# The last two token groups of the second FFN run alternately, chunk by chunk, and three instead of four steps at the border between the FFNs are in reversed order

## The chip, the core and the metric

The kernel runs on one core of a Trainium2 chip. The core has TensorE (PE in the profile; its weight loads are PEld), VectorE (DVE), ScalarE (ACT), GpSimd (POOL) and SyncE (SP), which issues the transfers here. Each engine takes its instructions in the order in which they are written; semaphores tie the engines together. Matrix products land in PSUM (8 banks), everything else lies in SBUF. The metric is the device time of one execution in microseconds, as the median of several runs.

## The reference, cut to what matters

```python
def reference(...):
    attn_out = _attn_ref(q_l, k_l, v_l, q_g, k_g, v_g)      # windowed attention with global tokens
    x = attn_out.transpose(0, 2, 1, 3).reshape(B * S, H * D)   # 2176 x 512
    x = _moe_ref(x, w_in, w_out)
    return _moe2_ref(x, w_in, w_out, a, b)

def _moe_ref(x, w_in, w_out):            # first FFN, 512 -> 2048 -> 512
    h = x @ w_in
    r = np.maximum(h, 0.0)
    return ((r * r) @ w_out).astype(np.float32)

def _moe2_ref(x, w_in, w_out, a, b):     # second FFN, the same shapes
    h = x @ w_in
    P = a[0] + a[1] * h + a[2] * h**2 + a[3] * h**3
    Q = 1.0 + np.abs(b[0]) * np.abs(h) + np.abs(b[1]) * h**2
    return ((P / (Q + 1e-06)) @ w_out).astype(np.float32)
```

## The kernel before

Attention comes first, with part of the first FFN filled in beside it; then the rest of the first FFN and the whole second one run as a list of jobs. A job is one chunk `f` of 128 of the 2048 hidden features for one group of tokens. Every matrix operand is split into a rounded part, hi, and what is left, lo, and a product is three matmuls (hi by hi, hi by lo, lo by hi).

The second FFN (`ph` 1) has six groups: five of 384 tokens and a last one of 256, `GRP[1]`, with 16 chunks each. `jobs` lists them group by group. N1 is the number of the first job of the second FFN, and all its weights are in SBUF when it is under way.

`step(k)` writes what belongs to step k, and there is no other scheduler: each engine's queue is the order of the code.

- `do_h(k)`, L314: 12 matmuls, hidden chunk k in one of two PSUM banks named S. The weights are stationary and the tokens move, so their width is 384 or 256. It is called h below.
- `x_split`, L296 and L297: one of the four 128-feature slices of a group's input is split into hi (ScalarE) and lo (VectorE). It needs a free slot out of `x_free`. There are five slots in the buffer `big`; two more (`x_more`, tiles `xm`) lie in the four word buffers `T` through which weights were converted before, each of 128 x 512 words, two to a slot. `step` looks ahead by 10, 7, 4 and 1 jobs to the first job of a group and splits one slice, at a distance of 1 all that are missing. `do_h` gives the slots back at a group's last chunk.
- `do_y(j)` for the job three steps back, L394: for each block of 128 tokens three matmuls 512 wide into a y bank; hi and lo of the chunk's result are stationary. First come all that need hi, two for each block, then one for each block that needs lo: 9 matmuls for 384 tokens, 6 for 256. It is called y. Six banks serve y, three or two for a group, in turn.
- `rat_a(k)`: three ScalarE functions (L350 to L352) and three VectorE operations (L353 to L355) for the chunk just computed. `rat_b(k - 1)`: Ln and Exp on ScalarE (L362, L363), then three VectorE operations (L364 to L366). `rat_c(k - 2)`: the copy to hi on ScalarE (L372), then lo on VectorE (L373).
- After a group's last y its banks are copied out, three or two ScalarE copies (L415), and each copy is sent to DRAM by SP (L416).

Within a step the order is h, x_split, y, then the three `rat` calls, then the output copies. The `rat` calls stand in the order a, b, c, except in the first four steps of the second FFN, where c comes first:

```python
        rat = [lambda op=op, d=d: op(k - d) for d, op in enumerate((rat_a, rat_b, rat_c)) if N1 <= k - d < NJ]
        for op in rat[::-1] if k < N1 + 4 else rat:
            op()
```

Of the kernel before, what the change touches and what calls it, by code (L numbers as in the profile page):

```python
# [10 lines left out]
F32R = mybir.dt.float32r  # L11
# [12 lines left out]
def kernel(  # L24
# [24 lines left out]
    NK = DM // 128  # L49
# [9 lines left out]
    NMAX = 384  # L59
# [6 lines left out]
    def bank(tag):  # L66
        i = turns[tag].pop(0)
        turns[tag].append(i)
        return ps.tile([128, 512], F32, tag=f"b{i}", name=tag)
# [162 lines left out]
    def cv_tick(left):  # L232

        cv["z"] += 1
        for it in line:
            it["age"] += 1
        if cv["z"] >= cv["per"] and len(todo) > left:
            cv["z"] = 0
            it = todo.pop()
            if it["mode"] == "both":  # L240
                w_back(it)
            else:
                it["age"], it["at"] = 0, cv["at"] if it["mode"] == "wide" else OS
                w_load(it)
                line.append(it)
        for nm in ORD:
            for it in line:
                if it["at"].get(nm) == it["age"]:
                    OPS[nm.replace("el", "l")](it)
        line[:] = [it for it in line if it["age"] < it["at"]["lo"]]  # L250

    def cv_idle():
        return not (todo or line)
# [5 lines left out]
    def row(i, r, n):  # L259
        return rows[i][:, NMAX * r:NMAX * r + n]  # L260

    x_free = [0, 1, 2, 3, 4]
    x_more = {}

    def x_slot(n):
        i = x_free.pop(0)
        pair = x_more[i] if i in x_more else [row(0, 2 * i + z, NMAX) for z in range(2)]
        return i, [x[:, 0:n].bitcast(F32R) for x in pair]

    def h_slot(n):  # L270
# [4 lines left out]
    groups_of = [[], []]  # L275
    t0 = NPART
# [5 lines left out]
    t0 = 0  # L282
# [2 lines left out]
        t0 += n  # L285
    jobs = []
    for ph in range(2):
        for gi, (t0, n, fs, add) in enumerate(groups_of[ph]):
            for f in fs:
                jobs.append((ph, gi, t0, n, f, f == fs[0], f == fs[-1], add))  # L290
    xs = {}

    def x_split(ph, gi, t0, n, k):
        i, (hi, lo) = x_slot(n)
        src = xT[:, k, t0:t0 + n]
        sc.copy(hi, src)  # L296
        ve.tensor_tensor(out=lo, in0=src, in1=hi.bitcast(F32), op=ALU.subtract)  # L297
        xs[ph, gi, k] = hi, lo, i
        if k == NK - 1 and groups_of[ph][gi][3]:
            sy.dma_start(xT[:, :, t0:t0 + n], park[:, :, t0:t0 + n])  # L300
# [3 lines left out]
    def do_h(j):  # L304
        ph, gi, t0, n, f, _, last, _ = jobs[j]
        w = wt[ph, f]
        h = bank("S")[:, 0:n]
        wk = [[w[:, s, 0, 128 * k:128 * k + 128] for s in range(2)] for k in range(NK)]
        x = [xs[ph, gi, k] for k in range(NK)]
        mm = [(k, s, 0) for k in range(NK) for s in range(2)] + [(k, 0, 1) for k in range(NK)]  # L310
        if last:
            mm = [(k, s, t) for k in range(NK) for s, t in ((0, 0), (1, 0), (0, 1))]
        for m, (k, s, t) in enumerate(mm):
            pe.matmul(h, wk[k][s], x[k][t], start=m == 0, stop=m == 3 * NK - 1)  # L314
        if last:
            x_free.extend(xs.pop((ph, gi, k))[2] for k in range(NK))
        hps[j] = h

    gs, mid = {}, {}
# [5 lines left out]
    def relu2(j, spare_ve):  # L325
        n = jobs[j][3]
        h = hps.pop(j)
        (hi, lo), g = h_slot(n)
        sc.activation(g, h, AF.Relu)  # L329
        gs[j] = hi, lo  # L330

        def square():
            sc.activation(hi, g, AF.Square)  # L333
            if spare_ve:
                sc.activation(g, g, AF.Square)
            else:
                ve.tensor_tensor(out=g, in0=g, in1=g, op=ALU.mult)  # L337

        def rest():
            ve.tensor_tensor(out=lo, in0=g, in1=hi.bitcast(F32), op=ALU.subtract)  # L340

        return square, rest
# [35 lines left out]
    def do_y(j):  # L378
        ph, gi, t0, n, f, st, sp, add = jobs[j]
        hi, lo = gs.pop(j)  # L380
        w = wt[ph, f]
        if st:
            yb[ph, gi] = [bank("y") for _ in range(NK if ph == 0 else n // 128)]
        y = yb[ph, gi]

        ms = range(len(y))
        for m, z in [(m, z) for m in ms for z in range(2)] + [(m, 2) for m in ms]:
            c = slice(128 * m, 128 * m + 128)
            if ph == 0:
                a, x = w[:, z % 2, 1, c], (hi, hi, lo)[z]  # L390
                pe.matmul(y[m][:, 0:n], a, x, start=st and z == 0, stop=sp and z == 2)  # L391
            else:
                a, x = (hi, hi, lo)[z][:, c], w[:, z % 2, 1]
                pe.matmul(y[m], a, x, start=st and z == 0, stop=sp and z == 2)  # L394

        def evac1(m):
            o = xT[:, m, t0:t0 + n]
            if add:
                ve.tensor_tensor(out=o, in0=y[m][:, 0:n], in1=o, op=ALU.add)
            else:  # L400
                (sc.copy if m % 2 else ve.tensor_copy)(o, y[m][:, 0:n])  # L401

        def evac():
            if ph == 0:
                for m in range(NK):
                    if j == N1 - 1 and m:
                        held.append(lambda m=m: evac1(m))
                    else:
                        evac1(m)
            else:  # L410
                for m in range(n // 128):

                    ks, c = ((slice(0, 2), 0), (slice(2, 4), 0), (slice(0, 4), 256))[m]
                    o = xT[:, ks, t0 + c:t0 + c + (128 if c else 256)]
                    sc.copy(o, y[m].rearrange("p (k t) -> p k t", t=o.shape[2]))  # L415
                    sy.dma_start(out[t0 + 128 * m:t0 + 128 * m + 128, :].rearrange("p (k t) -> p k t", t=o.shape[2]), o)  # L416

        if sp:
            outs.append(evac)

    NJ = len(jobs)
    N1 = sum(j[0] == 0 for j in jobs)
# [3 lines left out]
    def step(k):  # L426
        last, late = False, []

        if k < NR + 3:
            ticks, stage = (6 - (k > 5) if len(todo) > LEFT[2] else 2), (2 if k < NF else 3)  # L430
        elif k < N1 - (NF - NPRE) + 3:
            ticks, stage = 2, 4
        else:
            ticks, stage = (0 if cv_idle() else 6), 5
        left = LEFT[stage]
        if k < NJ:
            ph, gi, t0, n, f, _, last, _ = jobs[k]
            while (ph, f, 1) not in done:
                cv_tick(left)
            do_h(k)  # L440
        if k == N1:
            wide_s.close()
            pools["t"] = ctx.enter_context(tc.tile_pool(name="tmp", bufs=2, side="right"))
        if k >= N1 and not x_more and cv_idle():
            for i in (5, 6):
                x_more[i] = [cv3.tile([128, 512], U32, tag="T", name="xm").bitcast(F32) for _ in range(2)]
                x_free.append(i)
        for d in (1, 4, 7, 10):
            if k + d < NJ and jobs[k + d][5]:
                for z in range(NK):  # L450
                    if jobs[k + d][:2] + (z,) not in xs and x_free:
                        x_split(*jobs[k + d][:4], z)
                        if d > 1:
                            break


        lag = [2 if y < N1 else 3 for y in ys[:2]]
        if ys and ys[0] <= k - lag[0]:
            do_y(ys.pop(0))
            lag.pop(0)  # L460
        while ys and (ys[0] <= k - lag[0] or (last and lag[0] == 2 and ys[0] < k)):
            do_y(ys.pop(0))
            lag.pop(0)
            lag.append(2 if ys and ys[0] < N1 else 3)
        if k < NJ:
            if ph == 0:
                late = list(relu2(k, k < NF))
                ys.append(k)
        rat = [lambda op=op, d=d: op(k - d) for d, op in enumerate((rat_a, rat_b, rat_c)) if N1 <= k - d < NJ]
        for op in rat[::-1] if k < N1 + 4 else rat:  # L470
            op()
        if N1 <= k - 2 < NJ:
            ys.append(k - 2)
        while outs:
            outs.pop(0)()
        if held and k >= N1 + 6:
            held.pop(0)()

        for t in range(ticks):
            if late and t == 1:  # L480
                late.pop(0)()
            cv_tick(left)
        for f in late:
            f()


    fs = ctx.enter_context(ExitStack())
# [60 lines left out]
    with ExitStack() as at:  # L548
# [329 lines left out]
        for i in range(NS + 1):  # L878
# [13 lines left out]
            late = i + 2 < NS and groups[i + 2][1] == 4  # L892
# [30 lines left out]
            elif 0 <= fq < len(fjobs) - NPRE:  # L923
                a, f = fjobs[fq]
# [59 lines left out]
```

## Time and profile before

| | us |
|---|---|
| median of 3 runs (941.53 to 942.43) | 942.24 |
| profiled execution, its own time | 942.59 |
| its span, first to last instruction | 940.8 |
| PE busy | 903.2 (96%) |
| DVE busy | 727.1 (77%) |
| ACT busy | 618.5 (66%) |

The page of the profile cuts the span into 40 slices of 23.5 us and gives each engine's busy share in tenths (9 is 90% or more). In the second FFN, the last 17 slices or so, TensorE shows 9 in every slice but the last, VectorE 8 or 9, ScalarE 7 or 8. 81% of the chain that ended last lies on TensorE and 10% on VectorE. A timeline row gives the start of a group of like instructions in us from the span's start, how long it lasted, the engine, line and operation, and in brackets the idle time before it with what ended it. Durations include some overlap with the next instruction, so the spacing of starts tells how fast an engine goes on.

### The profile page before, as it was taken

To read this page: it belongs to the slowest core of one execution; us is meant where nothing else is said; L and a number is where in the kernel's file an instruction comes from. 1 tells how busy PE (TensorE), PEld (TensorE's weight loads), DVE (VectorE), ACT (ScalarE), POOL (GpSimd) and SP (SyncE) were. 2 spreads that over 40 slices of the span, in tenths; PEclk is the share of its full clock that TensorE was granted. 3 is DMA by queue.
4 is the path that set the end of the run, shared out by engine and by line. 5 is a ranking of instruction groups with operands and counts; after the bars stand their busy time and mean duration, and the time that the engine had idled before them with its cause. 6 is when DMAs were issued, how large, how long until landed. Compare 5 with 4: busy or idle time off the path is not lost.

```text
span 940.8 us, 19428 instructions
## 1 busy us (share of the span) xinstructions
PE 903.2 (96%) x7440; PEld 822.5 (87%) x7440; DVE 727.1 (77%) x1731; ACT 618.5 (66%) x1323; POOL 57.7 (6%) x109
## 2 busy tenths in 40 slices
PE   7878889999999999999999999999999999999997
PEld 4657788898999999999999988889889998988875
DVE  3599887765469577586766569989989999989886
ACT  3567475654578554555554557877888788787886
POOL 5233122210000000000000000000000000000000
PEclk9888999999999999999999999999999999999999
DMA  9997788730365264354522540010010010010000
GB/s 177 187 216 166 179 213 204 174 104 25 93 177 157 71 188 157 126 200 157 155 82 79 167 147 1 1 33 1 1 34 1 1 34 1 1 34 1 25 10 23
DMA packets 104301, 89.45 MB, mean 95 GB/s; under 512 B 60176, under 2 KB 87312, under 8 KB 104208
## 3 DMA queue, kind: packets, MB, share of 16 engines
q1 hardware_dynamic: 104208, 88.21, 35.2%
q8 instruction: 58, 0.95, 0.4%
q14 instruction: 35, 0.29, 0.1%
HBM read 62.13 MB, written 19.14 MB: 86 GB/s over the span
## 4 chain that ended last, share of the span: by engine, by line
PE 81%; DVE 10%; ACT 4%; DMA 3%; issue 1%; SPq 1%; ACTq 0%; DVEq 0%
PE S L314 33%; PE y L394 18%; PE y L391 15%; PE H L513 4%; PE Y L538 3%; PE S L733 2%; PE tr L700 1%; PE PV L827 1%; DVE T L168 1%; PE T L787 1%; DVE s L739 1%; DVE T L173 1%; DMA S<-in_moe_w_in_dram 1%; DMA big<-in_v_l_dram 1%; DVE tq L364 1%
## 5 line engine op out<-in xcount | busy, mean ns | idle before, releaser
L314 PE MATMUL S<-big,w 128*128 128x384 f32 (+1 forms) x1776 | 328.8, 326 | 2.1 <-ACT big L296 1.1
L314 PEld LDWEIGHTS S<-big,w 128*128 128x128 f32 x1776 | 296.5, 188 | 9.2 <-DVE ts L354 2.2
L394 PE MATMUL y<-w,big 128*128 128x512 f32 x816 | 209.1, 398 | 4.2 <-ACT big L372 2.9
L394 PEld LDWEIGHTS y<-w,big 128*128 128x128 f32 x816 | 149.3, 188 | 38.2 <-DVE big L373 8.1
L391 PE MATMUL y<-big,w 128*128 128x384 f32 (+1 forms) x912 | 159.6, 324 | 0.6 <-DVE xT L401 0.6
L391 PEld LDWEIGHTS y<-big,w 128*128 128x128 f32 x912 | 149.2, 188 | 1.5 <-DVE xT L401 1.0
L350 ACT ACTIVATE big<-S 128x384 f32<-128x384 f32 (+1 forms) x96 | 45.6, 475 | 75.4 <-PE S L314 72.1
L329 ACT ACTIVATE big<-S 128x384 f32<-128x384 f32 (+1 forms) x76 | 35.6, 468 | 81.9 <-PE S L314 81.9
L337 DVE TENSOR_TENSOR big<-big 128x384 f32<-128x384 f32 (+1 forms) x60 | 31.3, 522 | 71.2 <-ACT big L333 71.2
L353 DVE TENSOR_TENSOR ts<-ts,S 128x384 f32<-128x384 f32 (+1 forms) x96 | 50.9, 530 | 24.3 <-ACT ts L351 24.2
L314 PE MATMUL S<-xm,w 128*128 128x384 f32 (+1 forms) x288 | 67.8, 328 | 0.0
L352 ACT ACTIVATE tq<-big,coef 128x384 f32<-128x384 f32 (+1 forms) x96 | 66.1, 689 | 0.0
L351 ACT ACTIVATE ts<-S,coef 128x384 f32<-128x384 f32 (+1 forms) x96 | 62.5, 651 | 0.0
L354 DVE SCALAR_TENSOR_TENSOR ts<-ts,coef,S 128x384 f32<-128x384 f32 (+1 forms) x96 | 56.9, 593 | 3.4
L333 ACT ACTIVATE big<-big 128x384 fp32r<-128x384 f32 (+1 forms) x76 | 38.3, 504 | 29.6 <-PE y L391 29.1
L314 PEld LDWEIGHTS S<-xm,w 128*128 128x128 f32 x288 | 52.1, 188 | 2.9
L150 ACT ACTIVATE T<-S 128x512 f32<-128x512 f32 x64 | 42.7, 670 | 17.9 <-DMA S<-in_moe_w_in_dram 8.9
L366 DVE SCALAR_TENSOR_TENSOR ts<-tq,ts 128x384 f32<-128x384 f32 (+1 forms) x96 | 51.4, 536 | 3.3
L538 PE MATMUL Y<-f,w 128*128 128x256 f32 x360 | 51.3, 293 | 0.0
L513 PE MATMUL H<-f,w 128*128 128x256 f32 x360 | 51.0, 291 | 0.0
L373 DVE TENSOR_TENSOR big<-ts,big 128x384 fp32r<-128x384 f32 (+1 forms) x96 | 50.8, 529 | 0.2 <-ACT big L372 0.2
L355 DVE TENSOR_TENSOR tq<-tq,big 128x384 f32<-128x384 f32 (+1 forms) x96 | 50.8, 529 | 0.0
(131 smaller groups left out, 1314.2 us busy)
## 6 DMA issues: line engine op xcount, KB each, us to landing
S<-in_moe_w_out_dram SPq DMA_DIRECT2D x32, 512.0 KB, 4.5
S<-in_moe_w_in_dram SPq DMA_DIRECT2D x32, 256.0 KB, 4.5
S<-in_moe_w_in_dram SPq DMA_DIRECT2D x16, 512.0 KB, 4.5
scr<-T SPq DMA_DIRECT2D x24, 256.0 KB, 3.2
T<-scr SPq DMA_DIRECT2D x24, 256.0 KB, 2.7
both<-stg SPq DMA_DIRECT2D x10, 512.0 KB, 3.5
w<-both SPq DMA_DIRECT2D x10, 512.0 KB, 4.4
out_dram<-xT SPq DMA_DIRECT2D x17, 256.0 KB, 2.6
```

What stands on the lines that cost most here:

```text
L314: pe.matmul(h, wk[k][s], x[k][t], start=m == 0, stop=m == 3 * NK - 1)
L351: sc.activation(s, h, AF.Identity, scale=coef[:, 3:4], bias=coef[:, 2:3])
L352: sc.activation(q, av, AF.Identity, scale=coef[:, 7:8], bias=coef[:, 6:7])
L353: ve.tensor_tensor(out=s, in0=s, in1=h, op=ALU.mult)
L354: ve.scalar_tensor_tensor(out=s, in0=s, scalar=coef[:, 1:2], in1=h, op0=ALU.add, op1=ALU.mult)
L355: ve.tensor_tensor(out=q, in0=q, in1=av, op=ALU.mult)
L366: ve.scalar_tensor_tensor(out=s, in0=q, scalar=2.0, in1=s, op0=ALU.subtract, op1=ALU.mult, reverse0=True)
L373: ve.tensor_tensor(out=lo, in0=s, in1=hi.bitcast(F32), op=ALU.subtract)
L391: pe.matmul(y[m][:, 0:n], a, x, start=st and z == 0, stop=sp and z == 2)
L394: pe.matmul(y[m], a, x, start=st and z == 0, stop=sp and z == 2)
L513: pe.matmul(h, w[:, s, 0, 128 * k:128 * k + 128], fx[a, k][t], start=m == 0, stop=m == 3 * NK - 1)
L538: pe.matmul(fy[m // 2][:, NSUB * (m % 2):NSUB * (m % 2) + NSUB], w[:, z % 2, 1, 128 * m:128 * m + 128], (hi, hi, lo)[z], start=f == 0 and ...
```

## The change

Three things are written differently.

The list of jobs: the fifth group of 384 tokens and the group of 256 are one run, in which for each chunk first the 384 tokens and then the 256 stand. The 16 chunks thus become 16 pairs of jobs. All else follows from the list: h alternates between the groups, y three steps later does too, and both groups end with the last pair, their five y banks being copied out one after the other.

The input slots: since both groups hold their inputs at the same time, the small one gets all four slices into the two `xm` slots, hi and lo of a slice side by side in one word buffer of 2 x 256. The fourth and fifth groups may use only the five `big` slots (`x_room`), and the second FFN takes the highest free slot instead of the oldest.

The reversed order of the `rat` calls holds for three steps of the second FFN, not four.

```diff
--- before.py
+++ after.py
@@ -262,9 +262,22 @@
     x_free = [0, 1, 2, 3, 4]
     x_more = {}
 
-    def x_slot(n):
-        i = x_free.pop(0)
-        pair = x_more[i] if i in x_more else [row(0, 2 * i + z, NMAX) for z in range(2)]
+    def x_room(ph, gi):
+        late = len(groups_of[1]) - gi if ph else 9
+        return [i for i in x_free if (i < 5 if late in (2, 3) else i >= 5 if late == 1 else True)]
+
+    def x_slot(ph, gi, n, z):
+        last = ph == 1 and gi == len(groups_of[1]) - 1
+        i = max(x_room(ph, gi)) if ph else x_free[0]
+        if last:
+            t = x_more[5 + z // 2][z % 2]
+            pair = [t[:, 0:n], t[:, n:2 * n]]
+            if z % 2 == 0:
+                return None, [x.bitcast(F32R) for x in pair]
+            i = 5 + z // 2
+        else:
+            pair = x_more[i] if i in x_more else [row(0, 2 * i + z, NMAX) for z in range(2)]
+        x_free.remove(i)
         return i, [x[:, 0:n].bitcast(F32R) for x in pair]
 
     def h_slot(n):
@@ -285,13 +298,19 @@
         t0 += n
     jobs = []
     for ph in range(2):
-        for gi, (t0, n, fs, add) in enumerate(groups_of[ph]):
+        runs = [[gi] for gi in range(len(groups_of[ph]))]
+        if ph:
+            runs[-2:] = [runs[-2] + runs[-1]]
+        for run in runs:
+            fs = groups_of[ph][run[0]][2]
             for f in fs:
-                jobs.append((ph, gi, t0, n, f, f == fs[0], f == fs[-1], add))
+                for gi in run:
+                    t0, n, _, add = groups_of[ph][gi]
+                    jobs.append((ph, gi, t0, n, f, f == fs[0], f == fs[-1], add))
     xs = {}
 
     def x_split(ph, gi, t0, n, k):
-        i, (hi, lo) = x_slot(n)
+        i, (hi, lo) = x_slot(ph, gi, n, k)
         src = xT[:, k, t0:t0 + n]
         sc.copy(hi, src)
         ve.tensor_tensor(out=lo, in0=src, in1=hi.bitcast(F32), op=ALU.subtract)
@@ -313,7 +332,7 @@
         for m, (k, s, t) in enumerate(mm):
             pe.matmul(h, wk[k][s], x[k][t], start=m == 0, stop=m == 3 * NK - 1)
         if last:
-            x_free.extend(xs.pop((ph, gi, k))[2] for k in range(NK))
+            x_free.extend(i for i in [xs.pop((ph, gi, k))[2] for k in range(NK)] if i is not None)
         hps[j] = h
 
     gs, mid = {}, {}
@@ -448,7 +467,7 @@
         for d in (1, 4, 7, 10):
             if k + d < NJ and jobs[k + d][5]:
                 for z in range(NK):
-                    if jobs[k + d][:2] + (z,) not in xs and x_free:
+                    if jobs[k + d][:2] + (z,) not in xs and x_room(*jobs[k + d][:2]):
                         x_split(*jobs[k + d][:4], z)
                         if d > 1:
                             break
@@ -467,7 +486,7 @@
                 late = list(relu2(k, k < NF))
                 ys.append(k)
         rat = [lambda op=op, d=d: op(k - d) for d, op in enumerate((rat_a, rat_b, rat_c)) if N1 <= k - d < NJ]
-        for op in rat[::-1] if k < N1 + 4 else rat:
+        for op in rat[::-1] if k < N1 + 3 else rat:
             op()
         if N1 <= k - 2 < NJ:
             ys.append(k - 2)
```

What it makes of the queues, at three places. (Line numbers after the change are 19 higher: L333 is h, L413 y, L369 to L371 `rat_a`, L381 and L382 Ln and Exp, L391 the hi copy, L315 `x_split`. In the rows w is a weight chunk, S an h bank, y an output bank; big_4383 and xm hold inputs, big_4384 hi and lo of results; big_4385, ts, tq and tr are temporaries, coef and lnb constants.)

TensorE in the last group, before: h of 256 tokens (S<-...) and y of six matmuls by turns.

```order
L314 MATMUL S<-xm,w_7282 128x256 x2
L314 MATMUL S<-big_4383,w_7282 128x256 x6
L314 MATMUL S<-xm,w_7282 128x256
L314 MATMUL S<-big_4383,w_7282 128x256 x3
L394 MATMUL y<-w_7161,big_4384 128x512 x6
L314 MATMUL S<-xm,w_7313 128x256 x2
L314 MATMUL S<-big_4383,w_7313 128x256 x6
L314 MATMUL S<-xm,w_7313 128x256
L314 MATMUL S<-big_4383,w_7313 128x256 x3
L394 MATMUL y<-w_7199,big_4384 128x512 x6
```

TensorE at the same chunks, after:

```order
L333 MATMUL S<-big_4383,w_7282 128x384 x12
L413 MATMUL y<-w_7199,big_4384 128x512 x6
L333 MATMUL S<-xm,w_7282 128x256 x12
L413 MATMUL y<-w_7229,big_4384 128x512 x9
L333 MATMUL S<-big_4383,w_7313 128x384 x12
L413 MATMUL y<-w_7229,big_4384 128x512 x6
```

What moved: h is by turns 384 and 256 wide, and behind the h of one group stands the y of the other, so six matmuls behind the wide h and nine behind the narrow one.

ScalarE there, one step of the last group before (the three functions of `rat_a`, Ln and Exp of `rat_b`, the hi copy of `rat_c`):

```order
L350 ACTIVATE big_4385<-S 128x256
L351 ACTIVATE ts<-S,coef 128x256
L352 ACTIVATE tq<-big_4385,coef 128x256
L362 ACTIVATE big_4385<-tq,lnb 128x256
L363 ACTIVATE big_4385<-big_4385,lnb 128x256
L372 CAST big_4384<-ts 128x256
```

ScalarE, one step of 384 and one of 256 tokens, after:

```order
L369 ACTIVATE big_4385<-S 128x384
L370 ACTIVATE ts<-S,coef 128x384
L371 ACTIVATE tq<-big_4385,coef 128x384
L381 ACTIVATE tr<-tq,lnb 128x256
L382 ACTIVATE tr<-tr,lnb 128x256
L391 CAST big_4384<-ts 128x384
L369 ACTIVATE big_4385<-S 128x256
L370 ACTIVATE ts<-S,coef 128x256
L371 ACTIVATE tq<-big_4385,coef 128x256
L381 ACTIVATE big_4385<-tq,lnb 128x384
L382 ACTIVATE big_4385<-big_4385,lnb 128x384
L391 CAST big_4384<-ts 128x256
```

What moved: behind the three wide functions stand Ln and Exp of the 256 tokens and the wide hi copy, and in the next step the other way round.

ScalarE where the fifth group's inputs are split at the fourth group's last chunk, before:

```order
L372 CAST big_4384<-ts 128x384
L296 CAST xm<-xT 128x384
L350 ACTIVATE big_4385<-S 128x384
L351 ACTIVATE ts<-S,coef 128x384
L352 ACTIVATE tq<-big_4385,coef 128x384
L362 ACTIVATE big_4385<-tq,lnb 128x384
L363 ACTIVATE big_4385<-big_4385,lnb 128x384
L372 CAST big_4384<-ts 128x384
```

The same place after:

```order
L391 CAST big_4384<-ts 128x384
L315 CAST big_4383<-xT 128x384 x3
L369 ACTIVATE big_4385<-S 128x384
L370 ACTIVATE ts<-S,coef 128x384
L371 ACTIVATE tq<-big_4385,coef 128x384
L381 ACTIVATE big_4385<-tq,lnb 128x384
L382 ACTIVATE big_4385<-big_4385,lnb 128x384
L391 CAST big_4384<-ts 128x384
L315 CAST xm<-xT 128x256
L369 ACTIVATE big_4385<-S 128x384
```

What moved: three copies of 384 tokens (L315) stand ahead of the last chunk's functions instead of one, and one copy of 256 tokens ahead of the next step's.

ScalarE at the border between the FFNs, before, from the hi copy of the second chunk on:

```order
L372 CAST big_4384<-ts 128x384
L362 ACTIVATE big_4385<-tq,lnb 128x384
L363 ACTIVATE big_4385<-big_4385,lnb 128x384
L350 ACTIVATE big_4385<-S 128x384
L351 ACTIVATE ts<-S,coef 128x384
L352 ACTIVATE tq<-big_4385,coef 128x384
L350 ACTIVATE big_4385<-S 128x384
L351 ACTIVATE ts<-S,coef 128x384
L352 ACTIVATE tq<-big_4385,coef 128x384
L362 ACTIVATE tr<-tq,lnb 128x384
L363 ACTIVATE tr<-tr,lnb 128x384
L372 CAST big_4384<-ts 128x384
```

After, from the hi copy of the first chunk on:

```order
L391 CAST big_4384<-ts 128x384
L381 ACTIVATE tr<-tq,lnb 128x384
L382 ACTIVATE tr<-tr,lnb 128x384
L369 ACTIVATE big_4385<-S 128x384
L370 ACTIVATE ts<-S,coef 128x384
L371 ACTIVATE tq<-big_4385,coef 128x384
L369 ACTIVATE big_4385<-S 128x384
L370 ACTIVATE ts<-S,coef 128x384
L371 ACTIVATE tq<-big_4385,coef 128x384
L381 ACTIVATE big_4385<-tq,lnb 128x384
L382 ACTIVATE big_4385<-big_4385,lnb 128x384
L391 CAST big_4384<-ts 128x384
```

What moved: the second chunk's hi copy and the third chunk's Ln and Exp stand behind the fourth chunk's three functions instead of ahead of them.

## Rows read from the trace of the kernel before

**Rows 1.** Windows: stretch, us, then each engine's busy us (instructions), clock, DMA.

```profile
831.00:873.00 42.00, 42.00 (x212) 37.71 (x211) 38.73 (x75) 32.76 (x64) 0.00 (x0) 1.00 0.00 1
896.42:927.02 30.60, 29.81 (x180) 24.88 (x180) 27.49 (x71) 24.79 (x60) 0.00 (x0) 1.00 0.00 1
```

**Rows 2.** Timeline, TensorE, 384-token chunks: start us, us, operation, out<-in.

```profile
870.39 1.20 PE L314 MATMUL S<-big,w 128*128 128x384 f32 x6
...
872.47 2.25 PE L394 MATMUL y<-w,big 128*128 128x512 f32 x9
874.56 1.72 PE L314 MATMUL S<-big,w 128*128 128x384 f32 x9
```

**Rows 3.** ScalarE in time order, the same 384-token step.

```profile
872.67 0.49 ACT L350 ACTIVATE big<-S 128x384 f32<-128x384 f32 x1 [0.96 <-PE S L314]
...
874.21 0.61 ACT L362 ACTIVATE tr<-tq,lnb 128x384 f32<-128x384 f32 x1
...
875.38 0.49 ACT L372 CAST big<-ts 128x384 fp32r<-128x384 f32 x1
```

**Rows 4.** ScalarE in time order, a step of 256 tokens.

```profile
899.11 0.50 ACT L362 ACTIVATE big<-tq,lnb 128x256 f32<-128x256 f32 x1
899.64 0.51 ACT L363 ACTIVATE big<-big,lnb 128x256 f32<-128x256 f32 x1
900.06 0.39 ACT L372 CAST big<-ts 128x256 fp32r<-128x256 f32 x1
```

**Rows 5.** VectorE in time order, a step of 384 and one of 256 tokens.

```profile
874.87 0.55 DVE L355 TENSOR_TENSOR tq<-tq,big 128x384 f32<-128x384 f32 x1
...
900.19 0.42 DVE L364 SCALAR_TENSOR_TENSOR tq<-tq,big 128x256 f32<-128x256 f32 x1 [0.16 <-ACT big L363]
...
901.39 0.42 DVE L373 TENSOR_TENSOR big<-ts,big 128x256 fp32r<-128x256 f32 x1
```

**Rows 6.** Timeline, TensorE, 256 tokens (in brackets: idle time, releaser).

```profile
897.68 1.55 PE L394 MATMUL y<-w,big 128*128 128x512 f32 x6
899.08 0.40 PE L314 MATMUL S<-xm,w 128*128 128x256 f32 x2
...
900.50 1.20 PE L394 MATMUL y<-w,big 128*128 128x512 f32 x4
901.86 0.73 PE L394 MATMUL y<-w,big 128*128 128x512 f32 x2 [0.16 <-DVE big L373]
902.43 0.39 PE L314 MATMUL S<-xm,w 128*128 128x256 f32 x2
```

**Rows 7.** ScalarE in time order, the output copies of the fifth group.

```profile
890.26 1.55 ACT L415 COPY xT<-y 128x512 f32<-128x512 f32 x3
```

**Rows 8.** VectorE, then TensorE, in time order, where the fifth group ends.

```profile
877.10 0.55 DVE L373 TENSOR_TENSOR big<-ts,big 128x384 fp32r<-128x384 f32 x1
877.57 0.42 DVE L297 TENSOR_TENSOR big<-xT,big 128x256 fp32r<-128x256 f32 x1
...
880.16 2.70 PE L394 MATMUL y<-w,big 128*128 128x512 f32 x9
```

**Rows 9.** TensorE, then ScalarE, in time order, at the border between the FFNs.

```profile
565.55 2.75 PE L394 MATMUL y<-w,big 128*128 128x512 f32 x9 [1.42 <-ACT big L372]
568.14 2.29 PE L314 MATMUL S<-big,w 128*128 128x384 f32 x12
...
562.30 0.49 ACT L350 ACTIVATE big<-S 128x384 f32<-128x384 f32 x1 [1.85 <-DVE tq L355]
```

**Rows 10.** ScalarE and SP in time order: fifth group's start, last chunk, output.

```profile
814.06 0.49 ACT L350 ACTIVATE big<-S 128x384 f32<-128x384 f32 x1 [0.97 <-PE S L314]
...
928.63 0.39 ACT L350 ACTIVATE big<-S 128x256 f32<-128x256 f32 x1 [0.74 <-PE S L314]
...
936.06 1.07 ACT L415 COPY xT<-y 128x512 f32<-128x512 f32 x2 [1.83 <-PE y L394]
936.67 1.20 SPq L416 DMA_DIRECT2D out_dram<-xT  x2
```

## The prediction, made before the changed kernel was run

> **What bounds the kernel now.** I read the busy shares of two stretches first, then the instructions of TensorE, ScalarE and VectorE in order of time there, then the chain that ended last. In a stretch of 384-token chunks of the second FFN TensorE is busy all of the time, 42.00 of 42.00 us [rows 1]. One step is h (2.08 us, start to start) and y (2.09), with rounding 4.18 [rows 2]. In the last group, with 256 tokens, h takes 1.42 and y 1.40 [rows 6], but ten steps take 30.60 us, 3.06 each, of which TensorE is busy 29.81, VectorE 27.49 and ScalarE 24.79 [rows 1]. None of them is full: a chain through all three sets the end. It shows in TensorE's wait for VectorE's lo before the last third of a y [rows 6]. So a 384 and a 256 chunk cost 4.18 + 3.06 = 7.24 us now, of which TensorE needs 4.17 + 2.82 = 6.99. Running them alternately can at best give back 0.25 us for each pair; the question is whether the waits go.
>
> **The pair, worked out.** I write B for the 384 chunk and s for the 256 chunk. In a B step TensorE does h of B, then y of the s begun three steps before; in the s step it does h of s, then y of the B begun three steps before. ScalarE's queue in the B step is: three functions of the new B (L350 to L352), Ln and Exp of the s before it, and last the hi copy of the B two steps back. That copy is what y in the s step starts with. Clock zero is ScalarE's first function of B.
>
> TensorE: the y behind h of B starts 0.20 before zero (872.47 against 872.67) [rows 2, 3]; 1.40 for y of s and 1.42 for h of s [rows 6] bring it to y of B at 2.62.
>
> ScalarE: from the first function to Ln 1.54 (872.67 to 874.21) [rows 3]; Ln to Exp of 256 tokens 0.53, Exp to hi copy 0.42 [rows 4]; the hi copy of 384 tokens 0.49 [rows 3]; the handover to TensorE 0.05 (lo ends at 901.39 + 0.42, y goes on at 901.86) [rows 5, 6]. Sum 3.03: **TensorE waits 0.41 us** before y of B.
>
> VectorE: the third operation of B starts at 2.20 (874.87 against 872.67) [rows 3, 5] and the next can start 0.47 to 0.48 later (877.10 to 877.57 is such a neighbour) [rows 8], at 2.68; the three operations of s take 1.20 until lo starts (900.19 to 901.39) [rows 5]; lo of 384 tokens 0.55 and the handover 0.05: lo is there at 4.48. TensorE wants it at 3.03 + 1.40 + 0.10 = 4.53, so it just hides. (0.10 is what a restart costs: two matmuls from 901.86 to 902.43 take 0.57, and an undisturbed y of six takes 1.40, so two of it 0.47 [rows 6].)
>
> Then y of B ends at 3.03 + 2.09 + 0.10 = 5.22, the next h of B starts, and its first function follows 2.28 later (870.39 to 872.67) [rows 2, 3]: **a pair takes 7.50 us, not 7.24**. The s half adds no wait: its six operations on ScalarE follow B's at about 2.9, take some 2.8, and are done at 5.7, for a y that starts at 5.22 + 2.08 = 7.30; VectorE's seven end near 7.6, and their lo is wanted 0.93 after that y starts, at 8.2. Ends: 7.40 without a restart cost; 7.62 if lo misses and a second restart is paid.
>
> **The edge into the pairs.** The word buffers are kept for the small group, so three of the four inputs of the fifth 384 group are split at the last chunk of the fourth, where now one is, and the others three steps apart. Each takes VectorE 0.47 [rows 8]. VectorE idles 0.33 a step ((42.00 - 38.73) / 10) [rows 1], and by the same placing as above lo has about 0.4 of room in a step of 384; three splits are 1.4. ScalarE's third copy also waits for h's last matmuls, whose buffer it takes, and pushes its functions back by 0.4. Placed by these durations lo is 0.67 late, and in the next step, with one more split of 256 tokens, 0.50. A y of 2.70 instead of 2.25 at 880.16 is such a wait, of 0.45, after a single split [rows 8]. Taken 1.2, ends 0 and 2.5. The third group's border has two splits in a step instead of one: taken 0.2, ends 0 and 0.5.
>
> **The output copies** of a group of 384 take ScalarE 1.55 (the fifth group's) [rows 7]. The fourth group's now fall between steps of 384; among the pairs they fall into an s step, in which ScalarE idles 1.8 (5.7 to 7.5). I find a lo 0.5 late once, of which 0.3 overlaps the wait of the pair: 0.2 is taken.
>
> **The sum along the path**, from the first function of the fifth group (814.06) to the first output copy (936.06): 122.0 us before [rows 10]. After: the first pair, still with two y of the fourth group, 2.08 + 1.42 + 2 x 2.09 = 7.68 and 1.2 of waits, 8.9; the second, with one such y and so more cover, 7.7; the other 13 gaps between 16 B chunks at 7.50, and the 0.2, 97.7; from the last B on: VectorE ends the lo of the last s but one at 7.6, 0.57 for what is left of its y, 2.09 and 1.40 for the last two, and 0.1 to the copy, 11.8 (before, the same end took 7.43 from 928.63 [rows 10] and lies in the 122.0). Together 126.1, **4.1 us more**.
>
> **The output at the end** is five transfers instead of two. SP issues one in 0.60 (1.20 for two) [rows 10]. Now the last issue ends 1.8 after the first copy; five issues start some 1.6 earlier and end 2.0 after that point: +0.2, ends 0 and 0.5.
>
> **The border between the FFNs.** With three reversed steps instead of four, the second chunk's hi copy comes behind the fourth chunk's functions, but the third chunk's then no longer stands behind a backlog. Now ScalarE waits 1.85 for VectorE, y of the third chunk waits 1.42 and loses 0.5 in lo, and the next h starts at 568.14 [rows 9]. Placing the new order with the durations above, y of the second chunk starts 1.5 later than it does now and waits a little for lo, h runs from 563.5 to 565.6, y of the third chunk finds hi and lo ready and ends at 567.65: **-0.5**. Ends: -1.4 (that wait gone, nothing in its place) and +0.3.
>
> Sum: 4.1 + 0.2 + 0.2 - 0.5 = **+4.0 us**. The profiled execution is at 942.59 (span 940.8 and 1.8 around it), 0.35 above the median; it would go to 946.6, and the median from 942.24 to **946.2**.
>
> **Rivals.** *The waits go and TensorE is full (faster).* Then a pair takes 6.99, 13 x 0.51 = 6.6 less than forecast: 939.6. For it: no engine has more than 7 us of work in a pair, VectorE 3.87 + 2.75 = 6.6 [rows 1]. Against it: ScalarE's queue in the B step, under which lie only y and h of the small chunk. It decides from where the hi copy is ready 2.62 us after B's first function instead of 3.03. The Trainium skill (Perfetto Trace Analysis, Optimization Strategy) says that where the most-contended engine changes between stretches, interleaving those stretches may help; by that rule this rival would come true. The trace agrees only in part, since in the 256 stretch no engine is full by the busy times above.
>
> *About the same.* If the 256-token operations close up behind the 384 ones by 0.16 to 0.45 a pair, pairs take 7.05 to 7.34 and the time lies within 0.2% (1.9 us, about what a measurement of this kernel can tell), near 943.
>
> *Both waits show (slower still).* lo has 0.05 us of room. If it comes 0.2 later than placed, each pair pays that and a second restart of 0.10: 13 x 0.3 = 3.9, 950.1. In the pure 256 stretch lo is the late one [rows 6]; against it, the wait for hi gives it time.
>
> **Chances.** Forecast 0.64 (944.2 to 948.4: the pair gives -1.3 to +1.6, the edges -1.4 to +1.6, the border -0.9 to +0.8, which will not all fall to one side), both waits 0.12, same 0.13, faster 0.11. The range 943.8 to 949.0 leaves out the faster rival, most of the slowest and little else. Faster by over 0.2% 0.11, within it 0.13, slower 0.76.
>
> **What would show it.** In the last 110 us TensorE stops about 0.4 us before nearly every y of nine matmuls, released by ScalarE's hi copy; the first function of 384 tokens recurs every 7.5 us; at the edge two y wait for lo; after the FFN border the h that stood at 568.14 comes half a microsecond earlier. A recurrence near 7.0 without such a stop, or stops for VectorE in every y of nine, would make the forecast wrong, as would an edge that costs more than 2.5.

## The result and the profile after

The changed kernel takes 949.25 us (median of 8 runs, 944.09 to 950.97) where the kernel before took 942.26 in the same round: a ratio of 1.0061, 95% interval 1.0041 to 1.0082 (the two medians alone give 1.0074). In the round in which it ran beside three other kernels the ratio was 1.0050 (1.0032 to 1.0067). It is slower, as forecast; the median lies 0.25 us above the upper end of the range of the prediction, 949.0, and by the ratio the time is 948.0, inside it.

The single times scatter by several microseconds, before and after, so the second FFN is also compared by itself: from the first h at the border between the FFNs (a timeline piece of 24 matmuls) to the end of the span. In before that stretch is 397.43 us, from 543.37 to 940.8; after, from 542.82 to 945.6, it is 402.78, **5.35 us more**.

What the prediction called a pair, TensorE in time order near the end, after (start us, us, operation, in brackets idle time before it and what ended it):

```profile
922.05 1.58 PE L333 MATMUL S<-xm,w 128*128 128x256 f32 x12
923.90 2.39 PE L413 MATMUL y<-w,big 128*128 128x512 f32 x9 [0.27 <-ACT big L391]
926.13 2.27 PE L333 MATMUL S<-big,w 128*128 128x384 f32 x12
928.25 1.55 PE L413 MATMUL y<-w,big 128*128 128x512 f32 x6
929.63 1.58 PE L333 MATMUL S<-xm,w 128*128 128x256 f32 x12
931.49 2.40 PE L413 MATMUL y<-w,big 128*128 128x512 f32 x9 [0.27 <-ACT big L391]
```

The wide y (x9) stands behind the narrow h (1.42 long, start to start) and starts at 931.49, where that h was through at 931.05. It is released by ScalarE's hi copy (L391, before L372). In ScalarE's queue of the same step:

```profile
928.44 0.49 ACT L369 ACTIVATE big<-S 128x384 f32<-128x384 f32 x1 [1.91 <-PE S L333]
...
929.99 0.50 ACT L381 ACTIVATE tr<-tq,lnb 128x256 f32<-128x256 f32 x1
930.52 0.51 ACT L382 ACTIVATE tr<-tr,lnb 128x256 f32<-128x256 f32 x1
930.94 0.50 ACT L391 CAST big<-ts 128x384 fp32r<-128x384 f32 x1
```

From the first function of a 384 chunk to the hi copy in the same step, which is that of the 384 chunk before it, go 2.50 us, as the rows of before gave by adding up [rows 3, 4], and the copy ends at 931.44. The next chunk's first function came 7.58 us after the one before it, in each of the last 13 gaps (829.82 to 928.44: 7.58 to 7.60). So eight pairs take 60.6 us, of which TensorE is busy 58.46 (the columns are stretch, us, then PE, PEld, DVE, ACT and POOL busy, clock and DMA):

```profile
868.90:929.50 60.60, 58.46 (x313) 50.62 (x313) 50.38 (x112) 44.75 (x97) 0.00 (x0) 1.00 0.00 1
```

VectorE and ScalarE are less busy in that stretch than in the groups one after the other (50.38 and 44.75 of 60.60, so 0.83 and 0.74, against 0.92 and 0.78 in the 384 stretch of before [rows 1]): all wait in turn.

At the edge into the pairs, TensorE after:

```profile
813.14 1.55 PE L413 MATMUL y<-w,big 128*128 128x512 f32 x6
815.04 0.97 PE L413 MATMUL y<-w,big 128*128 128x512 f32 x3 [0.34 <-DVE big L392]
...
817.27 1.56 PE L413 MATMUL y<-w,big 128*128 128x512 f32 x6
819.02 0.97 PE L413 MATMUL y<-w,big 128*128 128x512 f32 x3 [0.20 <-DVE big L392]
```

Two y are cut in two, waiting for VectorE's lo: the first by 0.50 us (6 matmuls take 1.40, so 814.54 to 815.04), the second, at 819.02, by 0.35. Before, there was one such wait, in the row 880.16 [rows 8].

The border between the FFNs, TensorE after:

```profile
560.39 2.75 PE L413 MATMUL y<-w,big 128*128 128x512 f32 x9 [1.37 <-ACT big L391]
562.98 2.24 PE L333 MATMUL S<-big,w 128*128 128x384 f32 x12
...
567.14 2.27 PE L333 MATMUL S<-big,w 128*128 128x384 f32 x12
```

The wait of 1.4 has moved from the third chunk's y to the second's, and the h that starts at 567.14 is 24.32 behind the border's first h; in before it was 24.77 (543.37 to 568.14) [rows 9]. The end, ScalarE's copies and SP's transfers, and the share of the DMA engines' time in five stretches (the last two columns are that share and GB/s):

```profile
938.43 2.71 ACT L434 COPY xT<-y 128x512 f32<-128x512 f32 x5 [0.77 <-PE y L413]
939.04 3.25 SPq L435 DMA_DIRECT2D out_dram<-xT  x5
```

```profile
940.00:940.50 0.50, 0.26 (x2) 0.00 (x0) 0.00 (x0) 0.44 (x1) 0.00 (x0) 1.00 0.48 164
940.50:941.00 0.50, 0.00 (x0) 0.00 (x0) 0.00 (x0) 0.50 (x2) 0.00 (x0) 1.00 1.05 352
...
943.00:943.50 0.50, 0.00 (x0) 0.00 (x0) 0.00 (x0) 0.00 (x0) 0.00 (x0) 1.00 1.02 350
944.00:944.50 0.50, 0.00 (x0) 0.00 (x0) 0.00 (x0) 0.00 (x0) 0.00 (x0) 1.00 0.47 158
944.50:945.60 1.10, 0.00 (x0) 0.00 (x0) 0.00 (x0) 0.00 (x0) 0.00 (x0) 0.69 0.00 0
```

The transfers run without a gap from 940.2 to 944.3. From the small group's first copy (940.06, the fourth of the five) to the end of the span go 5.54 us; before it was 4.74, from 936.06 to 940.8 [rows 10].

### The profile page after: what moved, and what is told of

Same layout as the page of the kernel before. It is cut to its first block, busy times and chain, and to the rows that moved or that the text cites. A ratio compares the mean times of both kernels' runs of the same rounds, so it can differ in the third digit from the quotient of the medians.

```text
span 945.6 us, 19429 instructions
## 1 busy us (share of the span) xinstructions
PE 902.8 (95%) x7440; PEld 821.3 (87%) x7440; DVE 722.9 (76%) x1731; ACT 617.6 (65%) x1323; POOL 57.2 (6%) x109
## 4 chain that ended last, share of the span: by engine, by line
PE 77%; DVE 9%; ACT 6%; DMA 4%; SPq 1%; issue 1%; POOL 0%; ACTq 0%; DVEq 0%; POOLq 0%
PE S L333 31%; PE y L413 17%; PE y L410 15%; PE H L532 3%; PE Y L557 3%; PE S L752 2%; PE PV L846 1%; DMA S<-in_moe_w_in_dram 1%; DVE T L168 1%; PE tr L719 1%; ACT ts L370 1%; ACT tq L371 1%; PE T L806 1%; DVE T L173 1%; ACT big L369 1%
## 5 line engine op out<-in xcount | busy, mean ns | idle before, releaser
L333 PE MATMUL S<-big,w 128*128 128x384 f32 (+1 forms) x1728 | 319.8, 330 | 2.0 <-ACT big L315 1.1
L333 PEld LDWEIGHTS S<-big,w 128*128 128x128 f32 x1728 | 294.2, 188 | 8.6 <-DVE ts L373 1.6
L413 PE MATMUL y<-w,big 128*128 128x512 f32 x816 | 208.8, 398 | 6.8 <-ACT big L391 5.1
L413 PEld LDWEIGHTS y<-w,big 128*128 128x128 f32 x816 | 149.0, 188 | 42.4 <-ACT big L391 8.5
L369 ACT ACTIVATE big<-S 128x384 f32<-128x384 f32 x96 | 45.4, 473 | 82.9 <-PE S L333 81.0
L348 ACT ACTIVATE big<-S 128x384 f32<-128x384 f32 (+1 forms) x76 | 35.5, 467 | 82.1 <-PE S L333 82.1
L372 DVE TENSOR_TENSOR ts<-ts,S 128x384 f32<-128x384 f32 x96 | 50.8, 529 | 34.2 <-ACT ts L370 34.2
L371 ACT ACTIVATE tq<-big,coef 128x384 f32<-128x384 f32 x96 | 66.0, 688 | 0.0
L370 ACT ACTIVATE ts<-S,coef 128x384 f32<-128x384 f32 x96 | 62.4, 651 | 0.0
L333 PE MATMUL S<-xm,w 128*128 128x256 f32 (+1 forms) x336 | 60.7, 305 | 0.0
L373 DVE SCALAR_TENSOR_TENSOR ts<-ts,coef,S 128x384 f32<-128x384 f32 x96 | 56.9, 593 | 3.4
L385 DVE SCALAR_TENSOR_TENSOR ts<-tq,ts 128x384 f32<-128x384 f32 x96 | 51.4, 536 | 3.3
L333 PEld LDWEIGHTS S<-xm,w 128*128 128x128 f32 x336 | 51.2, 188 | 2.9
L374 DVE TENSOR_TENSOR tq<-tq,big 128x384 f32<-128x384 f32 x96 | 50.8, 529 | 0.0
L392 DVE TENSOR_TENSOR big<-ts,big 128x384 fp32r<-128x384 f32 x96 | 50.7, 528 | 0.1
```

What stands on the lines that cost most here:

```text
L369: sc.activation(av, h, AF.Abs)
L370: sc.activation(s, h, AF.Identity, scale=coef[:, 3:4], bias=coef[:, 2:3])
L371: sc.activation(q, av, AF.Identity, scale=coef[:, 7:8], bias=coef[:, 6:7])
L372: ve.tensor_tensor(out=s, in0=s, in1=h, op=ALU.mult)
L373: ve.scalar_tensor_tensor(out=s, in0=s, scalar=coef[:, 1:2], in1=h, op0=ALU.add, op1=ALU.mult)
L374: ve.tensor_tensor(out=q, in0=q, in1=av, op=ALU.mult)
```

## The experiments

The theory was the prediction's: the place of the hi copy in ScalarE's queue, behind Ln and Exp, makes TensorE wait once in every pair. The first rival: alternating widths costs on TensorE or VectorE itself. Further runs take the other terms of the sum one by one. All ratios are against the kernel before on the same chip; "stretch" is the one from the border's first h to the end of the span, in the profiled execution. The medians come from three rounds, in which the kernel before took 942.26 (the change), 943.39 (the four runs from "pairs only" to "groups, hi early in the last") and 944.18 (the change again, the outputs from two queues and the two "throughout"), so they compare through the ratios only. "hi early" stands for `rat_c` called ahead of `rat_b`.

| kernel | median us | ratio, 95% interval | stretch us |
|---|---|---|---|
| before | 942.26 | 1 | 397.43 |
| the change | 949.25 | 1.0061, 1.0041 to 1.0082 | 402.78 |
| the change again | 949.47 | 1.0050, 1.0032 to 1.0067 | 402.74 |
| pairs only | 947.98 | 1.0051, 1.0034 to 1.0067 | 403.04 |
| border only | 943.39 | 1.0003, 0.9987 to 1.0019 | 397.04 |
| pairs, hi early | 942.41 | 0.9991, 0.9975 to 1.0008 | 396.31 |
| groups, hi early in the last | 940.66 | 0.9971, 0.9955 to 0.9987 | 394.93 |
| the change without the edge's splits | 949.03 (one execution) | | 402.26 |
| the change, outputs from two queues | 951.06 | 1.0071, 1.0053 to 1.0088 | 402.81 |
| groups, hi early throughout | 937.82 | 0.9931, 0.9914 to 0.9948 | 391.93 |
| pairs, hi early throughout | 939.07 | 0.9942, 0.9924 to 0.9960 | 392.76 |

**`rat_c` earlier, pairs kept.** This moves the hi copy ahead of Ln and Exp on ScalarE, and lo ahead of the three operations of `rat_b` on VectorE. In the changed kernel:

```diff
-        rat = [lambda op=op, d=d: op(k - d) for d, op in enumerate((rat_a, rat_b, rat_c)) if N1 <= k - d < NJ]
+        abc = ((0, rat_a), (2, rat_c), (1, rat_b)) if k >= N1 + 66 else ((0, rat_a), (1, rat_b), (2, rat_c))
+        rat = [lambda op=op, d=d: op(k - d) for d, op in abc if N1 <= k - d < NJ]
```

> The changed kernel, but from the second pair on each step calls rat_c ahead of rat_b, so that ScalarE copies hi right behind the three functions, and VectorE does lo right behind its three operations, ahead of the work on Ln and Exp. My theory (the place of the hi copy in ScalarE's queue makes TensorE wait in every pair): hi of the 384 chunk is there 2.0 us after its functions begin instead of 3.0, TensorE wants it at 2.62, so the wait goes and a pair takes 7.0 instead of the 7.58 of the changed kernel; 13 gaps give 7.5 us, time 940 to 942. Rival (alternating widths costs on TensorE or VectorE itself, by weight loads or by lo): the period stays near 7.5 and the time within 1.5 us of the changed kernel.

TensorE in that kernel, where nothing is released by another engine any more:

```profile
903.91 2.26 PE L413 MATMUL y<-w,big 128*128 128x512 f32 x9
906.01 2.24 PE L333 MATMUL S<-big,w 128*128 128x384 f32 x12
908.09 1.55 PE L413 MATMUL y<-w,big 128*128 128x512 f32 x6
909.48 1.60 PE L333 MATMUL S<-xm,w 128*128 128x256 f32 x12
910.91 2.26 PE L413 MATMUL y<-w,big 128*128 128x512 f32 x9
```

The period is 7.01 us (903.91 to 910.91, y to y), against 7.58. The widths alternate as before, with the same work on every engine, so the rival falls: it was the order in the queues. The trace of the change names the hi copy as what TensorE waits for, but the run moves lo as well, and by the rows that too seems needed. VectorE's lo of the wide chunk in the change:

```profile
924.73 0.55 DVE L392 TENSOR_TENSOR big<-ts,big 128x384 fp32r<-128x384 f32 x1
```

It ends at 925.28. Without the wait for hi its y, now at 923.90, would have started at 923.47 (922.05 + 1.42) and asked for lo 1.40 later, at 924.87. That is an estimated 0.4 before lo is there. No run moves one of the two alone.

ScalarE in the run, the first function of a 384 chunk and the hi copy in the same step, then the hi copies at the very end:

```profile
908.29 0.49 ACT L369 ACTIVATE big<-S 128x384 f32<-128x384 f32 x1 [0.98 <-PE S L333]
...
909.83 0.51 ACT L391 CAST big<-ts 128x384 fp32r<-128x384 f32 x1
...
930.13 0.51 ACT L391 CAST big<-ts 128x384 fp32r<-128x384 f32 x1 [1.80 <-DVE ts L385]
...
932.99 0.41 ACT L391 CAST big<-ts 128x256 fp32r<-128x256 f32 x1 [1.41 <-DVE ts L385]
```

hi now starts 1.54 after the first function, not 2.50. The stretch is 6.47 shorter than in the change, though 13 gaps of 0.57 make 7.4: at the end, where no new chunk comes, hi waits 1.80 and 1.41 for VectorE in the two last chunks, where in the change it waits 0.59 and 1.01, and from the last 384 chunk's first function to the small group's first copy go 12.6 us (922.30 to 934.92) instead of 11.6.

**The same in the groups one after the other**, in the last group alone:

```diff
-        rat = [lambda op=op, d=d: op(k - d) for d, op in enumerate((rat_a, rat_b, rat_c)) if N1 <= k - d < NJ]
+        abc = ((0, rat_a), (2, rat_c), (1, rat_b)) if k >= N1 + 82 else ((0, rat_a), (1, rat_b), (2, rat_c))
+        rat = [lambda op=op, d=d: op(k - d) for d, op in abc if N1 <= k - d < NJ]
```

> The kernel before, with groups one after the other, but in the last group of 256 tokens rat_c ahead of rat_b from its third step on. My theory (the last group is bound by a chain in which lo comes last): steps of 256 tokens go from 3.06 to 2.82 to 2.90 us, TensorE's own time, so 2 to 3 us less than before, near 939.5, with no pairing at all. Rival (VectorE with 2.75 us of work and its bubbles is what binds there): steps stay at 3.0 to 3.06 and the time is that of before.

Ten steps of 256 tokens in that kernel (stretch, us, then busy us of PE, PEld, DVE, ACT):

```profile
896.53:924.50 27.97, 27.97 (x182) 25.24 (x181) 27.26 (x72) 25.90 (x61) 0.00 (x0) 1.00 0.00 1
```

They take 2.80 us each, not 3.06, and TensorE is busy throughout; VectorE does 27.26 of work in it, so the chain that bound the group [rows 6] was a matter of order as well, and VectorE would be next by these busy times. 2.50 us less in the stretch. A 384 and a 256 chunk now cost 4.18 + 2.80 = 6.98 one after the other, 7.01 as a pair: with the waits gone, alternating has nothing left to give in the steady part.

**Each half of the change alone.** The pairs with the old border, and the old groups with the new border:

```diff
-        for op in rat[::-1] if k < N1 + 3 else rat:
+        for op in rat[::-1] if k < N1 + 4 else rat:
```

> The paired order and the input slots of the change, with the border between the FFNs as it was before (four reversed steps). My theory of the parts: the border gives 0.5 us back in the change, so this should stand 0.5 us above the changed kernel, some 5.3 us in span above the kernel before. Rival: the border's change costs, then this one is faster than the changed kernel. In the trace the h after the third chunk's y should stand as late behind the border's first h as in before.

```diff
-        for op in rat[::-1] if k < N1 + 4 else rat:
+        for op in rat[::-1] if k < N1 + 3 else rat:
```

> The kernel before with three reversed steps at the border in place of four, nothing else. My theory: 0.5 us faster than before (ratio 0.9995), not to be told from no change in the times, but seen in the trace as a shorter stretch from the border's first h to the fifth chunk's h: 24.1 us against 24.6. Rival: no difference in that stretch, or a loss of up to 0.3.

The stretch from the border's first h to the seventh chunk's h (567.14 after, 568.14 before) is 24.76 us with the pairs and the old border, 24.41 with the groups and the new one, 24.32 in the change, 24.77 before. The new border gives 0.36 to 0.45 back, in either company, and the rest, 5.6 to 5.8, is the pairs'. In the times the border is not to be told from nothing, as expected. (The expectation's own numbers, 24.1 and 24.6, name the right difference, and its "fifth chunk" is the seventh.)

**The edge.** In `x_split`, the second to fourth slice of the fifth group are left out, so its tokens are computed from what lies in the slots:

```diff
-        sc.copy(hi, src)
-        ve.tensor_tensor(out=lo, in0=src, in1=hi.bitcast(F32), op=ALU.subtract)
+        if not (ph == 1 and gi == 4 and k):
+            sc.copy(hi, src)
+            ve.tensor_tensor(out=lo, in0=src, in1=hi.bitcast(F32), op=ALU.subtract)
```

> The changed kernel, in which the three splits of the fifth group that stand at the fourth group's last chunk are left out: its second to fourth input slices are not written, so its tokens are computed from what lies in the slots. My theory: the two waits for lo at the edge, of 0.5 and 0.4 us in the changed kernel's trace, come from these 1.4 us of VectorE and the late ScalarE copy; without them the first wait goes and the second shrinks to what one split of 256 tokens leaves, 0 to 0.3, so the stretch from the border's first h to the end is 0.6 to 1.0 shorter, 401.8 to 402.2 us against 402.8. Rival: these waits come from the narrower cover of the first pair alone, then both stay.

TensorE at the edge in that kernel:

```profile
815.35 2.25 PE L414 MATMUL y<-w,big 128*128 128x512 f32 x9
817.44 1.58 PE L334 MATMUL S<-xm,w 128*128 128x256 f32 x12
818.86 2.69 PE L414 MATMUL y<-w,big 128*128 128x512 f32 x9
821.39 2.27 PE L334 MATMUL S<-big,w 128*128 128x384 f32 x12
```

The first y is whole (2.09 to the next h). The second still loses 0.44 (2.53 instead of 2.09), more than the 0 to 0.3 expected; narrow cover and the single split of 256 tokens, as at the one of before [rows 8], are the likely cause, which no run takes apart. The stretch is 0.52 shorter, where 0.6 to 1.0 was expected. So the splits are worth 0.5, not the whole of what the edge lost.

**The end.** The small group's two transfers from ScalarE's queue:

```diff
-                    sy.dma_start(out[t0 + 128 * m:t0 + 128 * m + 128, :].rearrange(...), o)
+                    (sc if gi == 5 else sy).dma_start(out[t0 + 128 * m:t0 + 128 * m + 128, :].rearrange(...), o)
```

> The changed kernel, with the two output transfers of the small group issued from ScalarE's queue, so that SP issues three at the end and not five. My theory (the five transfers of 0.26 MB move one behind the other at about 335 GB/s, 3.9 us, and that sets the end): from the first copy of the small group to the end of the span 5.3 to 5.6 us, as in the changed kernel (5.54), no gain to be seen. Rival (SP's 0.6 us for each issue sets the end, the step of my prediction): 0.5 to 0.8 us less.

The two queues' rows of the last 16 us (packets, MB, share of 16 engines):

```profile
q1 hardware_dynamic: 1072, 0.79, 15.8%
q10 hardware_dynamic: 544, 0.52, 9.8%
```

The stretch is 402.81, as in the change, and the transfers take 15.8% and 9.8% of 16 us, 4.1 us in all, where the change's one queue took them in 4.1 as well (940.2 to 944.3). Issuing from ScalarE put its last copy some 0.7 behind (an issue of 0.64 stands between the copies), and the last issue ended 4.11 us behind the first copy (942.05 to 946.16) instead of 3.86 (938.43 to 942.29). Even that did not show at the end: the moving of 1.31 MB at about 320 GB/s sets it.

**The order throughout the second FFN**, for groups one after the other and for pairs, each with three reversed steps at the border:

```diff
-        rat = [lambda op=op, d=d: op(k - d) for d, op in enumerate((rat_a, rat_b, rat_c)) if N1 <= k - d < NJ]
+        abc = ((0, rat_a), (2, rat_c), (1, rat_b)) if k >= N1 + 3 else ((0, rat_a), (1, rat_b), (2, rat_c))
+        rat = [lambda op=op, d=d: op(k - d) for d, op in abc if N1 <= k - d < NJ]
```

> The kernel before, groups one after the other, with rat_c ahead of rat_b from the fourth step of the second FFN to its end, and three reversed steps ahead of that. My theory: the steps of 256 tokens at 2.80 us as in the kernel where only the last group had this order (2.5 us less than before), the border some 1.2 us shorter since the second chunk's hi copy no longer waits for Ln and Exp, and the waits behind the output copies (0.15 each, four times) and behind the last group's first split (0.45) gone: 4 to 5 us less than before, ratio 0.995 to 0.996. Rival: outside the last group TensorE is the bound and the order changes nothing there, then it equals the kernel with the order in the last group alone, ratio 0.997.

> The changed kernel with the same order as the run before this one. If pairing is worth something once no wait is left (rival), it should be at least as fast as the groups one after the other with that order. My theory: a pair takes 7.0 us and a 384 and a 256 chunk one after the other 6.98, so pairing gives nothing and keeps its edge and its five transfers at the end: 1 to 3 us slower than the groups one after the other with the same order, 2 to 3 us less than before.

The groups with this order beat both kernels: 0.9931 of before, stretch 391.93, 5.5 us less, where 4 to 5 was expected. TensorE at the border in it:

```profile
558.69 2.36 PE L314 MATMUL S<-big,w 128*128 128x384 f32 x12
561.30 2.37 PE L394 MATMUL y<-w,big 128*128 128x512 f32 x9 [0.25 <-ACT big L372]
563.50 2.29 PE L314 MATMUL S<-big,w 128*128 128x384 f32 x12
```

The second chunk's y waits a quarter of a microsecond instead of the 1.4 that it waits in the change, and the third's finds all ready: the seventh chunk's h stands 22.85 behind the border's first, 1.9 less than before. The pairs with the same order have a stretch of 392.76, 0.83 more, nearly all of it the 0.80 that their five transfers cost at the end. In the stretch the difference is less than the 1 to 3 us expected, since TensorE has no wait at the edge there either; the medians stand 1.25 apart.

**The change once more:**

> The changed kernel once more, unaltered, on the same chip as the next three. My theory: the second FFN costs 5.35 us more than before in every execution, and what the times scatter beyond that comes from the part ahead of it; the ratio should be near 1.0057, and the stretch from the border's first h to the end 402.8 us against 397.4. Rival: the change itself brings a slower kind of execution, with a median some 7 us above before and a second-FFN stretch that differs between profiles.

The stretch is 402.74, 402.78 and 402.81 in three executions with the same second FFN (the third with the outputs from two queues), while the border's first h comes anywhere from 542.4 to 546.5 in eleven profiles of all these kernels. So the rival falls: the change adds 5.35, and what the profiled executions show beyond it comes from ahead of the border, which the change does not touch. The medians are 7.0 above before in the first round and 5.3 in this one.

## Why the prediction came out as it did

**What bounds the kernel** was read rightly. That no engine was full in the last group, and a chain through them held it, is shown by the runs that only moved `rat_c`: the same work then takes 2.80 a step instead of 3.06.

**The pair** went as worked out, with the wait where it was put. It was 7.58 instead of 7.50: the handover and hi sum to 3.05 (3.03 predicted), y of nine after the restart takes 2.23 to the next h (2.19), that h 2.31 to the first function (2.28). Over 13 gaps that makes 1.1. The 0.2 for the output copies was not paid: lo came 0.49 late once (831.04 where 4 matmuls after 829.62 would have ended at 830.55), but all of it fell within the wait for hi, and that gap took 7.60. The room of 0.05 that the prediction saw for VectorE's lo held: no wide y of a steady pair is cut.

**The edge** waited twice, 0.50 and 0.35 where 0.67 and 0.50 were placed; the first pair took 8.77 (8.9), the second 7.71 (7.7), the drain 11.62 (11.8). The path from the fifth group's first function to the small group's first copy is 126.72 us (813.34 to 940.06), predicted 126.1, before 122.0.

**The third group's border**: from the seventh chunk to the fifth group's first function go 246.20 us (567.14 to 813.34), 245.92 before; 0.28 lost, 0.2 taken. The border's own step shows 0.11 of it (743.71 to the next h at 748.02, 4.31, where the same step before took 4.20); the rest builds up in small steps, mostly in the third group (4.20 instead of 4.17 from h to h in several), and its cause stays open. **The border between the FFNs** gave 0.45 (0.5 predicted).

**The output at the end** is where the prediction had the wrong limit. It let SP's issues set the end and took 0.2, with a bound of 0.5; it cost 0.80. The transfers themselves are the limit, as the two-queue run shows: 0.26 MB take about 0.8 us (4.1 for five), longer than an issue of 0.65 (3.25 for five). By the issues alone the end would have come some 0.4 earlier (an estimate: before, the span ends 2.93 after the last issue, after it 3.31), so about half of the 0.80 is issues, at 0.65 and not 0.60 each, and half the queue of transfers.

So the sum was 4.0 and the stretch shows 5.35: 0.6 from the path, 0.6 from the end, 0.1 from the two borders. Within the path the gaps' 0.9 met 0.1 less at the first pair and 0.2 less in the drain. In the profiled executions the time moved by 4.85 (942.59 to 947.44), because the part ahead happened to be 0.55 faster. Against the median of its own round the change stood at +7.0, which is more than the second FFN shows in any profile.

**The rivals.** TensorE full did not come true as long as the queues' order stayed: alternated, the two kinds of chunk took 7.58 where they had taken 7.24. With `rat_c` ahead they took 7.01 alternated and 6.98 apart. The Trainium skill (Perfetto Trace Analysis, Optimization Strategy) says that interleaving stretches with different most-contended engines may help. This case does not bear out the gain that the prediction drew from it, and the condition was not met: TensorE was the busiest engine in both stretches [rows 1], and in the second a chain held it. Neither "about the same" (pairs of 7.05 to 7.34) nor "both waits" happened.

## What to carry to other kernels

Before two loops are interleaved, find out whether the slower one is held by an engine or by the order in the engines' queues; the second is mended by moving instructions, and then interleaving may have nothing to give. When two widths alternate, check each wait again under the new cover: work of one width hides under work of the other, and here the wide hi copy had only the narrow step for cover. At the end of a kernel, count the bytes that are still to move, not only the issues.

## What the runs showed of the hardware beyond that

The scatter ahead of the border has a pace of its own. The same steps of the first FFN, 24 matmuls 384 wide with their weight loads, take 4.24 us in one execution and 4.16 in another, for whole stretches, with a granted clock of 1.00 in both and no wait. TensorE, first FFN, in the two-queue run, then in before:

```profile
425.65 2.28 PE L333 MATMUL S<-big,w 128*128 128x384 f32 x12
...
429.89 2.28 PE L333 MATMUL S<-big,w 128*128 128x384 f32 x12
```

```profile
428.68 2.24 PE L314 MATMUL S<-big,w 128*128 128x384 f32 x12
...
432.84 2.24 PE L314 MATMUL S<-big,w 128*128 128x384 f32 x12
```

From 425.65 to 429.89 and from 428.68 to 432.84. Up to the border 44 such steps follow one another (four groups of 11 chunks), so 0.08 each is 3.5 us, of the size of the scatter. Some executions change from one pace to the other between groups. It is not the whole scatter: in "groups, hi early throughout" and in "pairs only" the steps take 4.16 in all four groups, and yet the border's first h comes at 544.87 in one and at 542.36 in the other. What sets the pace, and the rest, stays open; no run here was made for it.
